# Moving weight and value loads, and splitting the first evacuation and the last accumulation, in a two-layer transformer kernel on one core

## The chip, the core and the metric

The kernel runs on one NeuronCore of a Trainium2 chip. The metric is the device time of one execution in microseconds. Times that are quoted as medians come from several executions; a profile is one execution, and its span (first to last event on the core) was 1.8 us shorter than the time of that same execution (1626.7 and 1628.48). All runs are fast: none was more than 1.5% above the fastest of its kernel.

Engines are named as the profile names them: PE is the tensor engine (matmuls), PEld its weight loads, DVE the vector engine, ACT the scalar engine, SP the engine that issues nearly all DMA transfers here, in program order (in the profile of before, all but two loads of `x`, 384 KB in sum, which ACT issues).

## The reference

Two identical layers run on 2048 tokens of width 1024, in bfloat16 (2 bytes a number). Each layer is attention and then a gated feed-forward block, each with a layernorm ahead and a residual add behind:

```python
def _A_ref(x, wqkv, wo):            # 32 heads of 32, window of 8 keys, 2 apart
    q, k, v = ...                   # (x @ wqkv), split
    kg, vg = k[..., idx, :], v[..., idx, :]        # idx = pos - (0, 2, ..., 14)
    logits = einsum("bhsd,bhswd->bhsw", q, kg) * scale     # masked where idx < 0
    o = einsum("bhsw,bhswd->bhsd", softmax(logits), vg)
    return o @ wo                   # (heads put back side by side)
def _B_ref(x, w1, w3, w2):          # width 3584
    return (silu(x @ w1) * (x @ w3)) @ w2
x = x + _A_ref(layernorm(x), A_wqkv, A_wo); x = x + _B_ref(layernorm(x), B_w1, B_w3, B_w2)
# ... and the same two lines once more
```

## The kernel before

PE does the matmuls. DVE does the whole windowed attention (multiplications and trees of additions), the norms and the residual adds. Tokens go in four chunks of 512; attention works on halves of a chunk (256 tokens). The program first makes q, k and v of chunks 0 to 3 of layer 0 (tile `ps`), with DVE doing attention of chunk 0 beside it; in chunk 3, four output projections (`po`) of chunk 0 are put between the `ps` matmuls; then the first feed-forward stage begins (`pg`, `pu`, then `acc`).

Instruction order on each engine is fixed when the program is built. A small model of time in the builder (`now`, `background`) decides where DVE's attention steps and the output projections go among the matmuls. A change of when a load is expected therefore also moves instructions.

q, k and v go through DRAM (`qkv_d`), since attention needs them in another cut. The value load is tried at the start of a half, when v is often not ready, and again after the softmax:

```python
for g, (l, h) in enumerate(halves):
    load_qk(l, h)
    ...
    load_v(l, h)                       # does nothing if v is not computed yet
    ...
    yield 0.0, ready, lambda: None
    yield from tree(W, mul_qk, lambda w_: psm[:, w_, :])       # scores
    NE = TCH // 32 * 8
    # ... softmax, 20 steps ...
    if g + 1 < len(halves):
        load_qk(*halves[g + 1])        # the next half's q and k
    load_v(l, h)                       # this half's v, behind them in the queue
```

The norm of the first four row blocks of chunk 0 is the program's start. PE transposes each normalized block into a tile that the program places in PSUM (`pT`), and ACT and DVE copy it from there to `xnT`, which the first `ps` matmuls read. These copies are called evacuations. `warm(n)` puts dummy matmuls between, so that PE isn't idle:

```python
kn = KT if j < 2 else KT // 2          # blocks per copy: 8, 8, 4, 4
...
copy = nc.vector.tensor_copy if h else nc.scalar.copy
```

The last accumulation of the program (12 matmuls of 512 columns), its residual add and its store are the program's end.

Of the kernel before, what the change touches and what calls it, by code (L numbers as in the profile page):

```python
# [15 lines left out]
def kernel(  # L16
# [13 lines left out]
    nc = tc.nc  # L30
# [58 lines left out]
    def pe(n, ready=0.0):  # L89
        now["pe"] = max(now["pe"], ready) + n * MM  # L90
        return now["pe"] + 0.1
# [52 lines left out]
    def bank(name):  # L144
        return psum.tile([P, 512], FP32, name=name, tag="mm")
# [24 lines left out]
    def warm(n):  # L170
        for i in range(n):
            pw = bank("pw")
            nc.tensor.matmul(pw[:], lhsT=hT[:, 0, 0:P], rhs=hT[:, 0, :], start=True, stop=True)
# [59 lines left out]
    def ln_first(key):  # L233


        xnT = xnTs[key] = xtp.tile([P, KT, CH], BF16, name="xnT")
        last = TPC - 1
        st = small.tile([P, last, 2, 6], FP32, name="st1", bufs=1)
        mv = small.tile([P, last, 2], FP32, name="mv1", bufs=1)
        sd = small.tile([P, TPC], FP32, name="sd1", bufs=1)  # L240
        rstd = small.tile([P, TPC], FP32, name="rstd1", bufs=1)
        am = small.tile([P, 3], FP32, name="am", bufs=1)
        junk = xnp.tile([P, D], BF16, name="xn")

        def stats(j, hh):
            nc.vector.bn_stats(st[:, j, hh, :], x_sb[:, j, hh * 512:(hh + 1) * 512])

        def deviation(j):
            if j < last:
                nc.vector.bn_aggr(mv[:, j, :], st[:, j, :, :])  # L250
                nc.scalar.activation(sd[:, j:j + 1], mv[:, j, 1:2], ACTF.Sqrt, bias=epst[:])
            else:
                nc.scalar.activation(sd[:, j:j + 1], am[:, 2:3], ACTF.Sqrt, bias=epst[:], scale=1.0 / D)

        def apply(j):
            nc.vector.reciprocal(rstd[:, j:j + 1], sd[:, j:j + 1])
            xn = xnp.tile([P, D], BF16, name="xn")
            if j < last:
                nc.vector.tensor_scalar(xn[:], x_sb[:, j, :], mv[:, j, 0:1], rstd[:, j:j + 1],
                                        op0=ALU.subtract, op1=ALU.mult)  # L260
            else:
                nc.vector.tensor_scalar(xn[:], x_sb[:, j, :], am[:, 1:2], rstd[:, j:j + 1],
                                        op0=ALU.add, op1=ALU.mult)
            kn = KT if j < 2 else KT // 2
            pTs = []
            for k0 in range(0, KT, kn):
                pT = psum.tile([P, kn, P], BF16, name="pT", tag="mm")
                for kk in range(k0, k0 + kn):
                    nc.tensor.transpose(pT[:, kk - k0, :], xn[:, kk * P:(kk + 1) * P], ident[:])
                pTs.append(pT)  # L270
            return pTs

        def evacuate(j, pTs):
            kn = KT // len(pTs)
            for h, pT in enumerate(pTs):
                copy = nc.vector.tensor_copy if h else nc.scalar.copy
                copy(xnT[:, h * kn:(h + 1) * kn, j * P:(j + 1) * P], pT[:])  # L277

        warm(NWARM)
        with hp(), tc.manual_schedule(engines={mybir.EngineType.PE, mybir.EngineType.DVE,  # L280
                                               mybir.EngineType.Activation}):
            stats(0, 0)
            stats(0, 1)
            deviation(0)
            stats(1, 0)
            nc.scalar.activation(junk[:], x_sb[:, last, :], ACTF.Copy, accum_out=am[:, 0:1])
            nc.scalar.mul(am[:, 1:2], am[:, 0:1], -1.0 / D)
            pT0 = apply(0)
            warm(4)
            stats(1, 1)  # L290
            deviation(1)
            nc.scalar.activation(junk[:], x_sb[:, last, :], ACTF.Square, bias=am[:, 1:2], accum_out=am[:, 2:3])
            stats(2, 0)
            pT1 = apply(1)
            warm(4)
            evacuate(0, pT0)
            deviation(last)
            stats(2, 1)
            deviation(2)
            evacuate(1, pT1)  # L300
            pT2 = apply(2)
            warm(2)
            pT3 = apply(3)
            evacuate(2, pT2)
            evacuate(3, pT3)
# [50 lines left out]
    def attention_steps():  # L356
# [3 lines left out]
        for g, (l, h) in enumerate(halves):  # L360
# [13 lines left out]

            yield 0.0, ready, lambda: None
            yield from tree(W, mul_qk, lambda w_: psm[:, w_, :])
            NE = TCH // 32 * 8
            psmT = smp.tile([P, W * NE, 4], BF16, name="psmT", tag="tr")
            L = smp.tile([P, W, NE], FP32, name="L", tag="L")
# [147 lines left out]
    def q_part(l, c, which, ws, then=()):  # L527

        ready = ready_norm(("Q", l, c))
        xnT = xnTs[("Q", l, c)]  # L530
        first = (l, c) == (0, 0) and which < 2
        if first:
            now_T = qkvp.tile([P, KT, TCH + (HALO if which else 0)], BF16, name="kT" if which else "qT")
            firsts.append(now_T)
            if which:
                nc.vector.memset(now_T[:, :, 0:HALO], 0.0)
        for t0 in range(0, KT, SG):
            sgt = stg.tile([P, SG, CH], BF16, name="sgt")
            for t in range(t0, t0 + SG):
                ps = bank("ps")  # L540
                for kk in range(KT):
                    nc.tensor.matmul(ps[:], lhsT=ws[kk // KH][:, kk % KH, t::KT], rhs=xnT[:, kk, :],  # L542
                                     start=(kk == 0), stop=(kk == KT - 1))
                r = pe(KT, ready)
                background(r)
                nc.scalar.copy(sgt[:, t - t0, :], ps[:])  # L546
                done = act(0.6, r)
                if first:
                    nc.scalar.copy(now_T[:, t, HALO if which else 0:], ps[:, 0:TCH])
                    done = act(0.4)  # L550
            nc.sync.dma_start(qkv_d[l][which][:, t0:t0 + SG, c * CH:(c + 1) * CH], sgt[:])
            between(False)
            if then and t0 // SG < len(then):
                then[t0 // SG]()
        qkv_at[l, c, which] = done + DMA / 2
        if len(firsts) == 2:
            qks[0, 0] = firsts[0], firsts[1], done + 0.1
            firsts.append(None)

    def b_stage(u, hold):  # L560
# [5 lines left out]
        for (f0, f1) in fsplits:  # L566
# [32 lines left out]
            for hh in range(2):  # L599
                w2ts = [weight("w2") for g0 in range(f0, f1, 8)]  # L600
                for j in range(TPC):
                    n = c * TPC + j
                    acc = bank("acc")
                    for f in range(f0, f1):
                        nc.tensor.matmul(acc[:], lhsT=hT[:, f - f0, j * P:(j + 1) * P],  # L605
                                         rhs=w2ts[(f - f0) // 8][:, (f - f0) % 8, :],
                                         start=(f == f0), stop=(f == f1 - 1))
                    pe(f1 - f0 - 1)
                    r = pe(1, th)
                    background(r + 1.0)  # L610
                    xs = x_sb[:, n, hh * 512:(hh + 1) * 512]
                    nc.vector.tensor_tensor(xs, xs, acc[:], op=ALU.add)  # L612
                    dve(0.64, r)
                    if last and lastsplit:
                        nc.sync.dma_start(xout[:, n, hh * 512:(hh + 1) * 512], xs)
                    if j == TPC - 1:
                        release(2)
                    between(hold and not lastsplit, lastsplit and hh == 0 and j == 1 and not hold)
# [15 lines left out]
    for c in range(NCH):  # L634
        for which in range(3):
            if c == NCH - 1 and which == 0:
                o_queue += [(0, n) for n in range(TPC)]
            if c == NCH - 1 and which == 2:
                between(False, True)
            then = ()  # L640
            if c == 0 and which == 0:
                then = (lambda: load_x(2), load_weight, load_weight, lambda: load_x(3))
            if c == 1 and which == 0:
                then = (load_weight, load_weight)
            if c == 1 and which == 1:
                then = (lambda: nc.sync.dma_start(wo[:], wo_v),)
            q_part(0, c, which, w_tiles[2 * which:2 * which + 2], then)
            if c == NCH - 1:
                release(2)
            if which == 0 and 1 <= c < NCH - 1:  # L650
                for r in range(R):
                    queue_norm(("Q", 0, c + 1), c + 1, r, (norm_apply,))
# [44 lines left out]
```

## Time and profile before

| reading | value | view |
|---|---|---|
| time, median of 3 | 1627.4 us (1626.39 to 1627.97) | runs |
| span of the profiled run | 1626.7 us | page |
| first projection matmul starts | 13.04 us | timeline of PE |
| one 512-column matmul to the next, streaming | 0.2158 us | timeline of PE |
| matmuls of 512 columns from there on | 7424, worth 1602 us | program |
| end of the last matmul to end of span | 3.5 us | timeline |

So only about 8 us of the stretch between the first and the last of these matmuls is not a stream of matmuls. Busy time doesn't show where it is lost. First, the waits of PE (who waited for whom: total in us, how often, longest).

```profile
PE po L500 <- DVE oT L319: 4.0, 2, 2.0
PE pT L269 <- DVE xn L259: 1.4, 2, 0.8
PE pw L173 <- DVE hT L166: 1.2, 1, 1.2
PE ps L542 <- ACT xnT L277: 0.5, 1, 0.5
```

The last three are in the first 13 us. The first is the third output projection. Its input `oT`, the output of attention, comes in eight slices, one for each matmul of an accumulation. Here it is in the timeline of PE (start, length, engine, line, operation, output and inputs, number; in brackets the idle time just before and what ended it).

```profile
164.98 1.34 PE L500 MATMUL po<-wo,oT 128*128 128x512 bf16 x5
168.33 0.39 PE L500 MATMUL po<-wo,oT 128*128 128x512 bf16 x1 [2.01 <-DVE oT L319]
170.73 4.68 PE L500 MATMUL po<-wo,oT 128*128 128x512 bf16 x10 [2.01 <-DVE oT L319]
...
200.26 1.89 PE L584 MATMUL pg<-xnT,w1t 128*128 128x512 bf16 x8
```

From 164.98 to the first `pg` at 200.26 lie 128 matmuls, which take 27.6 us when they stream. They took 35.3: the stall costs 7.65 us, although the waits name only 4.0. The table by windows shows the rest (window, its length, then busy us and count of PE, PEld, DVE, ACT and POOL, then the granted clock, that is, the clock at which PE was let run, as a share of full speed, DMA share and GB/s).

```profile
150.00:164.98 14.98, 14.87 (x69) 9.68 (x69) 14.80 (x29) 4.28 (x8) 0.00 (x0) 1.00 0.07 24
164.98:170.10 5.12, 1.73 (x7) 0.48 (x5) 5.05 (x10) 1.38 (x3) 0.00 (x0) 1.00 0.87 199
170.20:176.90 6.70, 6.11 (x14) 2.13 (x15) 6.63 (x13) 0.00 (x0) 0.00 (x0) 0.50 1.06 341
177.00:185.00 8.00, 7.95 (x38) 4.57 (x38) 6.80 (x12) 1.21 (x3) 0.00 (x0) 1.00 0.38 112
```

PE counts as 91% busy between 170.2 and 176.9, and yet it does half the work. The busy share doesn't show it; the clock column does, and so do the counts (15 weight loads in 6.7 us, and 38 in the 8.0 us after it). From 171.79 to 176.91 a weight load, and so a matmul, starts every 0.427 us (timeline of PEld), where the stream has one every 0.2158.

Why was `oT` late? DVE, which makes it, had waited for the values 90 us earlier (timeline of DVE, then of the DMA queue on SP).

```profile
80.93 0.11 DVE L335 MEMSET vT<- 128x64 uint32 x1
92.63 1.23 DVE L431 TENSOR_TENSOR tm<-At,vT 128x2048 bf16<-128x2048 bf16 x1 [11.59 <-DMA vT<-qkv_d]
```

```profile
76.44 0.47 SPq L646 DMA_DIRECT2D wo<-in_A_wo_dram  x1
77.00 2.82 SPq L551 DMA_DIRECT2D qkv_d<-sgt  x2
79.87 0.63 SPq L338 DMA_DIRECT2D qT<-qkv_d  x1
80.56 3.87 SPq L338 DMA_DIRECT2D kT<-qkv_d  x1
84.47 2.87 SPq L336 DMA_DIRECT2D vT<-qkv_d  x1
```

The value load is issued at 84.47, behind 2 MB of `wo` and behind q and k of the next half, and lands 8.1 us later. From 92.6 to 171 DVE is busy nearly all the time (76.4 of 78.4 us) and never catches up.

The start of the program, in the timeline of PE, is the third place:

```profile
11.98 0.61 PE L269 MATMUL pT<-ident,xn 128*128 128x128 bf16 x8
13.04 1.24 PE L542 MATMUL ps<-xnT,wqkv 128*128 128x512 bf16 x4 [0.45 <-ACT xnT L277]
```

The last entry of DVE before the end is the last residual add:

```profile
1623.23 0.69 DVE L612 TENSOR_TENSOR x_sb<-x_sb,acc 128x512 bf16<-128x512 bf16 x1 [1.90 <-PE acc L605]
```

### The profile page before, as it was taken

The page shows a single profiled execution, that of the slowest core. Times are in us where ns is not written, and L with a number is a line of the kernel's source. Part 1 is how long each engine was busy: PE and PEld are TensorE (multiplying, and loading weights), DVE is VectorE, ACT ScalarE, POOL GpSimd, SP SyncE. Part 2 cuts the span into 40 slices and gives each one's busy share as a digit, 9 for nine tenths or more (in the row PEclk, how much of TensorE's full clock was granted, in tenths as well). Part 3 has the DMA queues.
Part 4 walks back from the last instruction along what each step waited for, and adds up shares of the span by engine and source line. Part 5 has one row for each costly group of instructions (what it writes and reads, how often), then busy time and mean ns, then how long its engine had stood idle before and what let it go on. Part 6 is the DMA issues. An engine that isn't in the chain of part 4 may idle for free.

```text
span 1626.7 us, 18858 instructions
## 1 busy us (share of the span) xinstructions
PE 1608.2 (99%) x7330; PEld 801.3 (49%) x7479; DVE 1174.2 (72%) x1960; ACT 357.0 (22%) x558; POOL 1.9 (0%) x12
## 2 busy tenths in 40 slices
PE   9999899999999999999999999999999999999999
PEld 5666444444445644455444554445544444444444
DVE  5979998989898989998998439984489943122222
ACT  5432321123012330123312123021230212011110
POOL 0000000000000000000000000000000000000000
PEclk9999999999999999999999999999999999999999
DMA  9644766466547855577563676537775365436540
GB/s 316 185 148 117 209 194 184 139 184 183 169 130 213 254 155 168 168 203 240 157 182 130 207 233 167 178 124 239 227 208 162 99 194 169 142 104 220 156 129 27
DMA packets 335178, 285.28 MB, mean 175 GB/s; under 512 B 69616, under 2 KB 317680, under 8 KB 334960
## 3 DMA queue, kind: packets, MB, share of 16 engines
q1 hardware_dynamic: 334800, 283.67, 57.6%
q8 instruction: 58, 0.95, 0.2%
q10 hardware_dynamic: 288, 0.39, 0.1%
q14 instruction: 32, 0.26, 0.1%
HBM read 238.94 MB, written 29.36 MB: 165 GB/s over the span
## 4 chain that ended last, share of the span: by engine, by line
PE 93%; DVE 5%; DMA 1%; issue 1%; SPq 0%; ACT 0%; DVEq 0%
PE pu L592 24%; PE acc L605 24%; PE pg L584 24%; PE ps L542 15%; PE po L500 6%; DVE tm L431 1%; DVE tm L317 1%; DVE pr L372 1%; DMA vT<-qkv_d 0%; DVE pr L317 0%; SPq L338 0%; DMA x_sb<-in_A_x_dram 0%; DVE oT L319 0%; DVE xn L217 0%; DVE x_sb L505 0%
## 5 line engine op out<-in xcount | busy, mean ns | idle before, releaser
L592 PE MATMUL pu<-xnT,w3t 128*128 128x512 bf16 x1760 | 420.8, 379 | 2.1
L584 PE MATMUL pg<-xnT,w1t 128*128 128x512 bf16 x1751 | 419.2, 379 | 1.8
L605 PE MATMUL acc<-w2t,hT 128*128 128x512 bf16 x1757 | 387.7, 379 | 1.8
L542 PE MATMUL ps<-xnT,wqkv 128*128 128x512 bf16 x1506 | 332.1, 380 | 2.0 <-ACT xnT L277 0.5
L588 ACT ACTIVATE sg<-pg 128x512 bf16<-128x512 f32 x224 | 133.6, 597 | 767.3 <-PE pg L584 708.8
L596 DVE TENSOR_TENSOR hT<-sg,pu 128x512 bf16<-128x512 bf16 x224 | 152.7, 682 | 186.1 <-PE pu L592 174.2
L605 PEld LDWEIGHTS <-hT 128*128 128x128 bf16 x1792 | 175.4, 98 | 211.4
L584 PEld LDWEIGHTS <-w1t 128*128 128x128 bf16 x1792 | 175.4, 98 | 211.4
L592 PEld LDWEIGHTS <-w3t 128*128 128x128 bf16 x1792 | 175.3, 98 | 211.4
L542 PEld LDWEIGHTS <-wqkv 128*128 128x128 bf16 x1536 | 220.5, 144 | 113.0 <-issue 2.1
L372 DVE TENSOR_TENSOR pr<-qT,kT 128x2048 bf16<-128x2048 bf16 x128 | 156.3, 1221 | 88.6 <-DMA kT<-qkv_d 86.6
L431 DVE TENSOR_TENSOR tm<-At,vT 128x2048 bf16<-128x2048 bf16 x128 | 156.3, 1221 | 18.8 <-DMA vT<-qkv_d 16.5
L612 DVE TENSOR_TENSOR x_sb<-x_sb,acc 128x512 bf16<-128x512 bf16 x128 | 87.2, 681 | 103.3 <-PE acc L605 98.4
L546 ACT CAST sgt<-ps 128x512 bf16<-128x512 f32 x192 | 109.8, 587 | 236.5 <-PE ps L542 191.9
L317 DVE TENSOR_TENSOR pr<-pr 128x1024 bf16<-128x1024 bf16 (+1 forms) x256 | 134.5, 552 | 0.5
L317 DVE TENSOR_TENSOR tm<-tm 128x1024 bf16<-128x1024 bf16 (+1 forms) x256 | 134.2, 551 | 0.3
L500 PE MATMUL po<-wo,oT 128*128 128x512 bf16 x501 | 117.7, 384 | 4.7 <-DVE oT L319 4.0
L500 PEld LDWEIGHTS <-oT 128*128 128x128 bf16 x512 | 50.4, 99 | 66.1 <-DVE oT L319 5.6
L192 DVE BATCH_NORM_STATS2 st<-x_sb 128x6 f32<-128x512 bf16 x120 | 76.0, 672 | 6.9 <-DMA x_sb<-in_A_x_dram 6.9
L505 DVE TENSOR_TENSOR x_sb<-x_sb,po 128x512 bf16<-128x512 bf16 x64 | 43.3, 684 | 19.2 <-PE po L500 18.1
L588 ACT ACT_TABLE_LOAD x31 | 39.8, 1283 | 50.8 <-PE pg L584 46.6
L393 DVE STREAM_TRANSPOSE psmT<-psm 128x2048 bf16<-128x2048 bf16 x16 | 36.9, 2307 | 0.2
(88 smaller groups left out, 376.9 us busy)
## 6 DMA issues: line engine op xcount, KB each, us to landing
w1t<-in_B_w_dram SPq DMA_DIRECT2D x56, 1024.0 KB, 5.4
w3t<-in_B_w_dram SPq DMA_DIRECT2D x56, 1024.0 KB, 7.9
w2t<-in_B_w_dram SPq DMA_DIRECT2D x48, 1024.0 KB, 5.3
wqkv<-in_A_wqkv_dram SPq DMA_DIRECT2D x28, 1024.0 KB, 6.6
qkv_d<-sgt SPq DMA_DIRECT2D x96, 256.0 KB, 3.3
w2t<-in_B_w_dram SPq DMA_DIRECT2D x16, 512.0 KB, 5.1
qT<-qkv_d SPq DMA_DIRECT2D x15, 512.0 KB, 9.0
kT<-qkv_d SPq DMA_DIRECT2D x14, 544.0 KB, 9.8
```

The source lines that it names most:

```text
L317: nc.vector.tensor_tensor(b[:, 0:m, :], b[:, 0:m, :], b[:, m:2 * m, :], op=ALU.add)
L372: V.tensor_tensor(pr[:], qT[:], kT[:, :, k0:k0 + TCH], op=ALU.mult)
L431: V.tensor_tensor(tm[:], At[:], win, op=ALU.mult)
L500: nc.tensor.matmul(ps[:], lhsT=oT[:, t, j * P:(j + 1) * P], rhs=wo[:, t, hh * 512:(hh + 1) * 512], start=(t == 0), stop=(t == KT - 1))
L542: nc.tensor.matmul(ps[:], lhsT=ws[kk // KH][:, kk % KH, t::KT], rhs=xnT[:, kk, :], start=(kk == 0), stop=(kk == KT - 1))
L546: nc.scalar.copy(sgt[:, t - t0, :], ps[:])
L584: nc.tensor.matmul(pg[:], lhsT=w1t[:, kk, fi * P:(fi + 1) * P], rhs=xnT[:, kk, :], start=(kk == 0), stop=(kk == KT - 1))
L588: nc.scalar.activation(sg[:], pg[:], ACTF.Silu)
L592: nc.tensor.matmul(pu[:], lhsT=w3t[:, kk, fi * P:(fi + 1) * P], rhs=xnT[:, kk, :], start=(kk == 0), stop=(kk == KT - 1))
L596: nc.vector.tensor_tensor(hT[:, f - f0, :], sg[:], pu[:], op=ALU.mult)
L605: nc.tensor.matmul(acc[:], lhsT=hT[:, f - f0, j * P:(j + 1) * P], rhs=w2ts[(f - f0) // 8][:, (f - f0) % 8, :], start=(f == f0), stop=(f == ...
L612: nc.vector.tensor_tensor(xs, xs, acc[:], op=ALU.add)
```

## The change

Its intent: take weights that aren't needed yet out of the way of the values, ask for the values earlier, start the first projection sooner, and shorten the end. The diff, shortened: re-indented lines and most of its context are left out, and `# ...` marks what else is:

```diff
 # first norm: blocks per copy 8, 8, 8, 2 and another order
-            kn = KT if j < 2 else KT // 2
+            kn = (KT, KT, KT, KT // 4)[j]
-                copy = nc.vector.tensor_copy if h else nc.scalar.copy
+                copy = nc.vector.tensor_copy if j == 2 or h > 1 else nc.scalar.copy
-            evacuate(0, pT0)
             deviation(last)
             stats(2, 1)
             deviation(2)
+            evacuate(0, pT0)
             evacuate(1, pT1)
+            warm(2)
             pT2 = apply(2)
-            warm(2)
             pT3 = apply(3)
 # attention
             yield from tree(W, mul_qk, lambda w_: psm[:, w_, :])
+            load_v(l, h)
 # last accumulation, in two halves of 256 columns (`final` is true once)
+                    step = 256 if final else 512
+                    for q0 in range(0, 512, step):
+                        acc = psum.tile([P, step], FP32, name="acc", tag="mm")
+                        # ... 12 matmuls, add and store of these columns
 # loads beside the projections (one entry after each of the four groups of a part)
-            if then and t0 // SG < len(then):
+            if t0 // SG < len(then) and then[t0 // SG]:
                 then[t0 // SG]()
 # ...
-            if c == 1 and which == 0:
-                then = (load_weight, load_weight)
-            if c == 1 and which == 1:
-                then = (lambda: nc.sync.dma_start(wo[:], wo_v),)
+            if c == 2 and which == 0:
+                then = (None, None, lambda: nc.sync.dma_start(wo[:], wo_v))
+            if c == 2 and which == 1:
+                then = (load_weight, None, load_weight)
```

More of the change, by code (lines that the diff above doesn't have):

```diff
@@ L602, in b_stage @@
                     n = c * TPC + j
-                    acc = bank("acc")
-                    for f in range(f0, f1):
-                        nc.tensor.matmul(acc[:], lhsT=hT[:, f - f0, j * P:(j + 1) * P],
-                                         rhs=w2ts[(f - f0) // 8][:, (f - f0) % 8, :],
-                                         start=(f == f0), stop=(f == f1 - 1))
-                    pe(f1 - f0 - 1)
-                    r = pe(1, th)
-                    background(r + 1.0)
-                    xs = x_sb[:, n, hh * 512:(hh + 1) * 512]
-                    nc.vector.tensor_tensor(xs, xs, acc[:], op=ALU.add)
-                    dve(0.64, r)
-                    if last and lastsplit:
-                        nc.sync.dma_start(xout[:, n, hh * 512:(hh + 1) * 512], xs)
+                    final = u == len(units) - 1 and lastsplit and hh == 1 and j == TPC - 1
+                    step = 256 if final else 512
+                    for q0 in range(0, 512, step):
+                        acc = psum.tile([P, step], FP32, name="acc", tag="mm")
+                        for f in range(f0, f1):
+                            nc.tensor.matmul(acc[:], lhsT=hT[:, f - f0, j * P:(j + 1) * P],
+                                             rhs=w2ts[(f - f0) // 8][:, (f - f0) % 8, q0:q0 + step],
+                                             start=(f == f0), stop=(f == f1 - 1))
+                        if q0 == 0:
+                            pe(f1 - f0 - 1)
+                            r = pe(1, th)
+                            background(r + 1.0)
+                            dve(0.64, r)
+                        o0 = hh * 512 + q0
+                        xs = x_sb[:, n, o0:o0 + step]
+                        nc.vector.tensor_tensor(xs, xs, acc[:], op=ALU.add)
+                        if last and lastsplit:
+                            nc.sync.dma_start(xout[:, n, o0:o0 + step], xs)
                     if j == TPC - 1:
```

## The prediction

> **What bounds it.** TensorE. The page gives PE busy 99%, and the chain of waits that ended last is 93% PE. 7424 512-column matmuls at one per 0.2158 us (the trace's spacing) are 1602 us. The span is 1626.7: 13.04 before the first projection matmul, 1610.4 to the last matmul's end (1623.4), 3.3 of tail. So only 8.2 us inside the matmul stretch are not streaming. Waits of PE show one stall there: "po <- DVE oT", 4.0 us, near 166 to 171 us. The table by windows shows the granted clock at 0.50 from 170.4 to about 177, while po and ps go on at half rate. From the start of that output projection (164.98) to the first gate matmul (200.26) lie 128 matmuls, worth 27.6 us; they took 35.3. The stall therefore costs 7.65 us: 4 idle, 3.6 slow clock. [...]
>
> **Why oT is late.** VectorE is late: it idles 11.6 us (80.9 to 92.6) for vT, whose load stands in the DMA queue behind 2 MB of wo and behind qT and kT; after that VectorE is the chain up to 171.
>
> **What the change does.**
> 1. vT of the first half is now issued after the second chunk-1 query store (about 62.5 us) with w1, w3 and wo out of the way; lands about 70. VectorE reaches it at 81: the 11.6 us wait goes. wo (issued near 105, needed at 140) and w1/w3 (near 112 to 118, needed near 195) come in time.
> 2. The model that orders the program moves too: the third output projection stands one SG group (16 matmuls, 3.45 us) earlier, and one attention tree step (2.4 us) moves ahead of the first residual adds. Replaying trace durations, oT's last slice is ready near 160.5; PE starts that projection near 160.6 and needs the slice at 162. No stall, but only 1 to 2 us to spare. Gain 7.6.
> 3. First norm: sd of rows 2 no longer waits behind the first 0.99 us evacuation, so xn2, xn3 and the transposes come about 0.35 earlier; quarters let the first matmul start after a short copy. First projection matmul near 12.2 instead of 13.04. Gain 0.8 (ScalarE now runs the two big copies back to back, which limits it).
> 4. Tail: 12 extra matmuls, each half the width, about +0.05; last add 256 wide, 0.42 instead of 0.69, and a smaller last store. Gain 0.3 to 0.4.
> 5. Second layer: order shifts on VectorE, values loads earlier; PE had no wait there, so nothing.
>
> All gains lie on the critical path and add: 7.6 + 0.8 + 0.35 = 8.8. 1627.4 - 8.8 = 1618.6 us, range 1617.2 to 1621.3. Faster by over 2% 0.01, within 2% 0.985, slower by over 2% 0.005.
>
> **What would show it.** Right: no "tm <- DMA vT" wait near 81; no (or under 0.5 us) "po <- oT" wait; granted clock 1.00 throughout; first projection matmul at 12.0 to 12.4; first gate matmul near 191.8; last add about 0.4 us. Wrong: a po wait surviving at 160 to 165, PE waiting for wo near 140 or for w1 near 192, first matmul still near 13.
>
> **What would make it wrong.** VectorE's adds wait for po in the new order, so oT comes 2 us later than replayed and a stall of 1 to 3 us stays, perhaps with the half clock again (result 1621 to 1624). Stores held up behind the 2 MB wo load. A new order in the second layer that makes PE wait. The 256-column matmuls not hiding their weight loads (+0.3).

The sum: 7.6 + 0.8 + 0.35 = 8.8, and the 7.6 is read from the trace (35.28 less 27.62 us). The +0.05 for the halved matmuls and the +0.3 for their weight loads are guesses that name no source. Measured after the change, the adds of the two halves start 1.30 us after the add before them and 1.32 us apart (1612.19, 1613.49, 1614.81): 2.62 us for 24 matmuls of 256 columns, where 24 halves of 0.2158 make 2.59.

## The result, and the profile after

| | before | after |
|---|---|---|
| time, median | 1627.68 us (4 runs, 1626.39 to 1628.26) | 1619.63 us (4 runs, 1619.56 to 1619.73) |
| span of the profiled run | 1626.7 us | 1617.9 us |
| first projection matmul | 13.04 us | 12.20 us |
| first `pg` matmul | 200.26 us | 191.80 us |
| end of last matmul to end of span | 3.51 us | 3.13 us |

The ratio of times is 0.9952, with a 95% interval of 0.9934 to 0.9969: about 0.5% less, the class "same" by the 2% rule. A ratio is the mean time of one kernel's fast runs over that of the other's of the same rounds, so it isn't quite the ratio of the medians quoted.

The waits of PE after the change have no `po` line any more (line numbers are one higher from the attention on):

```profile
PE pw L173 <- DVE hT L166: 1.2, 1, 1.2
PE pT L269 <- DVE xn L259: 0.6, 1, 0.6
PE ps L543 <- DVE xnT L277: 0.3, 1, 0.3
```

The same places in the timeline of PE:

```profile
12.20 2.13 PE L543 MATMUL ps<-xnT,wqkv 128*128 128x512 bf16 x8 [0.33 <-DVE xnT L277]
...
160.72 3.62 PE L501 MATMUL po<-wo,oT 128*128 128x512 bf16 x15
164.18 3.62 PE L543 MATMUL ps<-xnT,wqkv 128*128 128x512 bf16 x16
...
191.80 1.89 PE L585 MATMUL pg<-xnT,w1t 128*128 128x512 bf16 x8
```

The third projection streams, and so does what follows; the windows show full clock:

```profile
160.72:164.18 3.46, 3.41 (x17) 1.61 (x17) 2.28 (x3) 0.59 (x1) 0.00 (x0) 1.00 0.85 248
164.18:171.08 6.90, 6.90 (x33) 3.87 (x32) 6.02 (x10) 1.17 (x2) 0.00 (x0) 1.00 1.02 340
```

The cause is gone where it began. The values are issued at 61.94 and land 4.5 us later, and DVE has no wait in front of its first multiplication with them (queue of SP, then DVE):

```profile
61.94 0.62 SPq L336 DMA_DIRECT2D vT<-qkv_d  x1
```

```profile
80.19 1.23 DVE L432 TENSOR_TENSOR tm<-At,vT 128x2048 bf16<-128x2048 bf16 x1
...
160.19 0.29 DVE L319 TENSOR_TENSOR oT<-tm 128x256 bf16<-128x256 bf16 x1
...
1613.49 0.42 DVE L619 TENSOR_TENSOR x_sb<-x_sb,acc 128x256 bf16<-128x256 bf16 x1 [0.62 <-PE acc L609]
1614.81 0.42 DVE L619 TENSOR_TENSOR x_sb<-x_sb,acc 128x256 bf16<-128x256 bf16 x1 [0.89 <-PE acc L609]
```

The last slice of `oT` is done at 160.48, 0.2 us before the projection that reads it starts and 1.7 us before its own matmul, the eighth (160.72 and seven times 0.2158). The last add takes 0.42 instead of 0.69 us.

### The profile page after: what moved, and what is told of

The parts are those of the page before. It is cut to its first block, busy times and chain, and to the rows that moved or that the text cites. A ratio compares the mean times of both kernels' runs of the same rounds, so it can differ in the third digit from the quotient of the medians.

```text
span 1617.9 us, 18887 instructions
## 1 busy us (share of the span) xinstructions
PE 1604.7 (99%) x7342; PEld 802.1 (50%) x7491; DVE 1176.1 (73%) x1962; ACT 358.8 (22%) x558; POOL 1.9 (0%) x12
## 4 chain that ended last, share of the span: by engine, by line
PE 98%; DVE 1%; issue 1%; DMA 0%; ACT 0%; SPq 0%; DVEq 0%
PE acc L609 24%; PE pu L593 23%; PE pg L585 23%; PE ps L543 20%; PE po L501 7%; DVE tm L432 0%; DMA x_sb<-in_A_x_dram 0%; DVE tm L317 0%; DVE hT L597 0%; DVE st L246 0%; DVE At L416 0%; DVE xn L259 0%; ACT xnT L277 0%; DVE xnT L277 0%; PE pT L269 0%
## 5 line engine op out<-in xcount | busy, mean ns | idle before, releaser
L609 PE MATMUL acc<-w2t,hT 128*128 128x512 bf16 (+1 forms) x1769 | 387.7, 378 | 1.8
L319 DVE TENSOR_TENSOR psm<-pr 128x256 bf16<-128x256 bf16 x128 | 36.7, 287 | 0.5
```

The costliest lines, as they stand in the source:

```text
L609: nc.tensor.matmul(acc[:], lhsT=hT[:, f - f0, j * P:(j + 1) * P], rhs=w2ts[(f - f0) // 8][:, (f - f0) % 8, q0:q0 + step], start=(f == f0), ...
```

## The experiments

Theory: nearly all of the gain is one stall, caused by the wait of DVE for the values, and it costs its idle time plus a period at half clock; head and tail add about 1.1 us on top. Rivals: the traffic of the weights and not the place of the value load is the cause; or the clock drop has another origin and only the waiting counts; or head and tail gains are eaten by later waits.

Since the first matmul's start moves by a few tenths from run to run with the landing of the first input (in the seven profiles with the head of the change it lies between 11.78 and 12.46, and always 6.19 to 6.25 after the first `xn`, which came at 5.58 to 6.21; DVE's waits ahead of that name the load of `x`), spans are compared below from the first projection matmul on, where that matters. The profile gives spans to 0.1 us, so such a difference is good to about 0.1 us.

| run | time, median us (lowest to highest) | span | first `ps` | span from first `ps` | `po` wait of PE | half clock |
|---|---|---|---|---|---|---|
| before | 1627.40 (1626.39 to 1627.97) | 1626.7 | 13.04 | 1613.66 | 4.0 | 170.2 to 177.0 |
| e1 values early | 1620.55 (1620.36 to 1620.55) | 1618.8 | 12.76 | 1606.04 | none | none |
| e2 weights later | 1622.02 (1621.60 to 1623.10) | 1619.8 | 12.52 | 1607.28 | 0.3 | none |
| e3 filled stall | 1625.79 (1625.14 to 1626.37) | 1623.8 | 12.95 | 1610.85 | 1.0 | none |
| e11 head and tail | 1626.57 (1626.14 to 1627.12) | 1625.1 | 12.33 | 1612.77 | 4.0 | 168.1 to 174.9 |
| e4 after again | 1619.48 (1619.47 to 1619.59) | 1617.7 | 11.97 | 1605.73 | none | none |
| e5 old head | 1620.22 (1620.18 to 1620.28) | 1618.5 | 12.84 | 1605.66 | none | none |
| e6 old tail | 1619.85 (1619.67 to 1620.12) | 1617.8 | 11.80 | 1606.00 | none | none |
| e7 finer both | 1619.77 (1619.27 to 1620.47) | 1617.9 | 11.56 | 1606.34 | none | none |
| e8 one more | 1619.49 (1619.46 to 1619.51) | 1617.7 | 11.98 | 1605.72 | none | none |
| e9 three more | 1621.60 (1621.59 to 1622.05) | 1620.3 | 12.46 | 1607.84 | 1.8 | none |
| e10 six more | 1628.02 (1627.19 to 1628.51) | 1625.4 | 11.78 | 1613.62 | 5.3 | 165.1 to 171.9 |
| e12 finer head | 1619.40 (1619.16 to 1619.43) | 1617.6 | 11.96 | 1605.64 | none | none |

e1, e2, e3 and e11 ran on one chip, where before had 1627.70; e4 to e7 together, with before at 1627.79; e8 to e10 together, with before at 1627.48; e12 alone, with before at 1627.13. All results were correct.

### e1: only the values earlier

```diff
 # the kernel before, with
             yield from tree(W, mul_qk, lambda w_: psm[:, w_, :])
+            load_v(l, h)
```

> The kernel before with only the new place of the values load (after the scores); wo, w1, w3 still load in chunk 1. Theory (the 11.6 us wait of VectorE for vT is the whole cause of the stall, and the place of the load in the queue is enough): the vT wait near 81 us is gone or under 1 us, no po <- oT wait, granted clock 1.00, span 7.6 us under that of before (1626.7), so about 1619. Rival (traffic of w1, w3 and wo is what delays vT): the wait for vT stays above 5 us, the stall stays, gain under 4 us.

The stall and the wait are gone although `w1`, `w3` and `wo` still load in chunk 1: from the first `ps` on the span is 1606.04, which is 7.6 us less than before (1613.66 less 1606.04). The value load is issued at 62.96, right behind 2 MB of `w1` and `w3`, and lands only after 8.2 us, as slowly as before (8.1). That doesn't matter, because DVE wants it at 80.7. The rival that traffic alone is the cause falls: being asked for 18 us early is enough. The edit also lets the builder's model put the third projection 16 matmuls earlier (161.25), as in the changed kernel, so e1 doesn't change the load alone; e2, which leaves the order as it was, shows that the new order isn't needed to lose the stall.

### e2: only the weights later

```diff
 # the kernel before, with the guard of `then` as in the change, and
-            if c == 1 and which == 0:
-                then = (load_weight, load_weight)
-            if c == 1 and which == 1:
-                then = (lambda: nc.sync.dma_start(wo[:], wo_v),)
+            if c == 2 and which == 0:
+                then = (None, None, lambda: nc.sync.dma_start(wo[:], wo_v))
+            if c == 2 and which == 1:
+                then = (load_weight, None, load_weight)
```

> The kernel before with only wo, w1, w3 moved into chunk 2; order of PE, VectorE, ScalarE unchanged, vT still issued after qT and kT. Theory (queue place and traffic each are enough): vT issued near 81, lands near 87, VectorE's wait 6 to 7 instead of 11.6 us, so oT about 5 us earlier, the stall at the third output projection 0 to 1 us and no half clock: gain 6.5 to 7.6 us. Rival (the queue place alone matters): wait for vT above 10 us, stall and half clock stay, gain under 1 us.

The order on PE, DVE and ACT is that of before. The values were issued at 80.77 and DVE's wait fell from 11.6 to 7.3 us, where 6 to 7 had been worked out; the `po` wait fell to 0.3 and the clock stayed at full speed. So traffic alone was also enough to lose the stall; the rival of the queue place alone falls too. But the gain in the median was 5.7 us (1627.70 less 1622.02), and 6.4 in the profiles from the first `ps` on, less than the 6.5 to 7.6 expected. A new wait shows, which the expectation hadn't seen:

```profile
193.38 1.89 PE L584 MATMUL pg<-xnT,w1t 128*128 128x512 bf16 x8 [0.56 <-issue]
```

The first feed-forward matmul reads `xnT` and `w1t`. `w1t` of this stage was issued at 121.8, long before. The last two transposes of `xnT` were issued only at this point in the DMA queue, behind 2 MB of weights issued from 181.79 on:

```profile
181.79 0.42 SPq L471 DMA_DIRECT2D w1t<-in_B_w_dram  x1
182.31 1.67 SPq L471 DMA_DIRECT2D w3t<-in_B_w_dram  x1
184.06 7.05 SPq L220 DMA_TRANSPOSE xnT<-xn  x2
```

The two transposes took the queue 7.05 us to issue, until 191.1. In the changed kernel the builder's model, which expects the values earlier, also puts the third and fourth output projections 16 matmuls earlier, and with them the adds and the norm; the same two transposes were issued from 176.09 on, in 2.69 us, 13 us before they were wanted. The second of the two was issued at 188.6 and took 4.5 us to land, until 193.1, 0.3 us before `pg` started. That the transposes are what `pg` waited for is read from their place and these times; the profile names no releaser, and no run took this wait away by itself. From the start of the third projection (164.47) to `pg`, e2 takes 1.3 us more than its 128 matmuls need: 0.55 for the last slice of `oT` (its matmul starts at 166.53) and the rest at `pg`. That is what e2 falls short of e1 from the first `ps` on (1607.28 less 1606.04).

### e3: the stall filled with dummy matmuls

```diff
 # the kernel before, in the output projection
         oT = oTs[l, h]
+        if (l, n) == (0, 2):
+            warm(16)
         for hh in range(2):
```

> The kernel before with 16 dummy matmuls (3.45 us) put just ahead of the third output projection, where PE would idle. Theory (the stall costs 4.0 us of idling and 3.6 us of half clock): granted clock stays 1.00, idle left under 1 us, the first gate matmul about 3.6 us earlier than before's 200.26, span near 1623.1. Rival (the cost is only the waiting, or the slow clock comes from something else such as power or DMA load): the first gate matmul stays at 200 or moves later by up to 3.4 us, and the clock drops in the same place.

Sixteen useless matmuls made the kernel faster: 1625.79 against 1627.70. The clock stayed at 1.00:

```profile
164.89 3.62 PE L173 MATMUL pw<-hT 128*128 128x512 bf16 x16
168.34 1.46 PE L502 MATMUL po<-wo,oT 128*128 128x512 bf16 x6
170.54 0.39 PE L502 MATMUL po<-wo,oT 128*128 128x512 bf16 x1 [0.73 <-DVE oT L319]
```

So the clock drop goes with PE being idle, and not with the DMA load of that time, which this run has too (DMA share 0.84 from 165.0 to 168.4 and 0.91 to 1.06 from there to 172.0, in windows of e3). The first `pg` was at 197.33, 2.93 us earlier than before, not 3.6, and from the first `ps` on the run was 2.8 us shorter. The expectation had taken the waiting from the list of waits, which ends with the next-to-last slice of `oT`. In the kernel before the last slice's matmul starts at 171.39 (its weight load is at that time in the timeline of PEld) and would have started at 166.49 if the projection had streamed from 164.98. So waiting costs 4.9 us. The half clock then lasts to 177.0 and costs half of the 5.6 us from there, 2.8. Together that is, within 0.1 us, the 7.65 that was read, and 2.8 is what e3 saved. The split of the prediction, 4 and 3.6, was wrong and its sum was right.

### e11: only head and tail

```diff
 # the kernel before, with
-            kn = KT if j < 2 else KT // 2
+            kn = (KT, KT, KT, KT // 4)[j]
 # ... and the other lines of the first norm in the change
+                    step = 256 if final else 512
 # ... and the loop over q0 of the change
```

> The kernel before with only the new first norm and the halved last accumulation. Theory (the parts add up): first projection matmul near 12.20 instead of 13.04, tail 0.3 us shorter, stall as in before; if VectorE in chunk 0 moves with PE, the stall stays near 4 us: gain 1.1 us in the span, and times vary between runs as those of before do. Rival: the earlier start makes PE reach the stall 0.84 us earlier while oT comes no earlier (VectorE's wait is set by the DMA queue), so the head's gain is eaten by a stall 0.84 us longer: gain only 0.3 us.

The gain in the median is 1.13 us (1627.70 less 1626.57), with the `po` wait unchanged at 4.0. The rival of a longer stall falls, but for a little: DVE's work moved with PE's, and the last slice's matmul (170.87) came 5.05 us late, where it was 4.9 before. The half clock fell differently (windows of this run):

```profile
165.80:168.00 2.20, 0.19 (x1) 0.10 (x1) 2.17 (x5) 0.37 (x1) 0.00 (x0) 1.00 1.06 199
168.10:174.90 6.80, 4.74 (x12) 1.64 (x12) 6.73 (x12) 0.00 (x0) 0.00 (x0) 0.50 1.04 327
```

The same stall now meets the drop 2.3 us after its beginning, not 3.8 as before, so the slow period covers 4.0 us of streaming work after the last slice (170.87 to 174.9) and not 5.6. Its cost is 2.0 and not 2.8 us. The cost of nearly the same stall thus varies with the moment at which the clock drops, 170.2 in before and 168.1 here.

### e4, e5, e6: the changed kernel again, with the old head, with the old tail

```diff
 # e5: the changed kernel with
-            kn = (KT, KT, KT, KT // 4)[j]
+            kn = KT if j < 2 else KT // 2
 # ... and the other lines of the first norm as before
 # e6: the changed kernel with
-                    step = 256 if final else 512
+                    step = 512
```

> The changed kernel again, as the base of the next three runs. Expected 1619.6 us with a spread under 0.4 us between runs, while the kernel before spreads over 1.5 to 2 us [...].

> The changed kernel with the old first norm. Theory: first projection matmul at 13.0 instead of 12.2, span 0.8 us longer (1618.7), time 1620.4. Rival (the head's gain is hidden by later waits): within 0.2 us of the changed kernel.

> The changed kernel with the old, unhalved last accumulation. Theory: last add 0.69 instead of 0.42 us and a larger last store: 0.2 to 0.4 us longer (span 1618.1 to 1618.3). Rival (extra matmuls and an extra store eat it): within 0.1 us or shorter.

The old head costs 0.74 us (1620.22 less 1619.48), all of it ahead of the first matmul: from there on the spans are 1605.66 and 1605.73. The old tail costs 0.37 in the medians, and 0.27 in the span from the first `ps` (1606.00 less 1605.73); the time from the last matmul's end is 3.46 and 3.15. Both rivals fall. The repeat of the changed kernel gave the same time within 0.15 us, with a spread of 0.12.

### e7 and e12: finer pieces

```diff
 # e7 and e12: the changed kernel with
-            kn = (KT, KT, KT, KT // 4)[j]
+            kn = (KT, KT, KT // 2, KT // 4)[j]
 # e7 only
-                    step = 256 if final else 512
+                    step = 128 if final else 512
```

> The changed kernel with the second-last evacuation of the first norm in halves (one on ScalarE, no: both by VectorE) and the last accumulation in quarters. Theory: the first projection matmul now waits for VectorE's 0.69 us copy; its half lets it start about 0.25 us earlier (near 11.95), and quarters save another 0.1 us of add and store: 0.2 to 0.4 us faster. Rival: ScalarE's two big copies set the start, so nothing at the head, and 128-wide matmuls are bound by their weight loads, so the tail loses 0.1 us or more.

> The changed kernel with the third row block of the first norm evacuated by VectorE in two halves, the last accumulation in halves as in the changed kernel. Theory (the first projection matmul waits for VectorE's 0.69 us copy of eight blocks, of which it needs one; the earlier run with quarters started earlier and lost that at the tail): first projection matmul 0.2 to 0.3 us earlier, no wait for a VectorE copy before it, tail as in the changed kernel, median 1619.2 to 1619.3 against 1619.5. Rival (that earlier start was only jitter of when the first input lands): 1619.5, same as the changed kernel.

e7 missed its expectation: the median is 0.3 us above the changed kernel's (1619.77 against 1619.48), not 0.2 to 0.4 below. Its head did gain (2.00 us from `xn` of the third block to the first `ps`, as in e12 below). The last add became shorter and the end longer: 3.74 us from the last matmul's end against 3.15. Matmuls weren't the cause; the DVE timeline shows three adds 0.67 us apart, so the 12 matmuls of 128 columns of each took 56 ns apiece. By the column that is within 4% of the 215.8 ns for 512 columns, so weight loads held them up by little at most.

```profile
1612.86 0.29 DVE L619 TENSOR_TENSOR x_sb<-x_sb,acc 128x128 bf16<-128x128 bf16 x1 [0.38 <-PE acc L609]
1613.53 0.29 DVE L619 TENSOR_TENSOR x_sb<-x_sb,acc 128x128 bf16<-128x128 bf16 x1 [0.38 <-PE acc L609]
1614.20 0.29 DVE L619 TENSOR_TENSOR x_sb<-x_sb,acc 128x128 bf16<-128x128 bf16 x1 [0.38 <-PE acc L609]
```

The stores were: the four of 32 KB took 3.7, 3.4, 2.9 and 2.4 us from issue to landing, where the two of 64 KB in the changed kernel took 1.5 and 1.6. The rows of the four are 256 bytes. What made the stores slow isn't shown: the 128 KB store just ahead of them, whose rows have 1024 bytes, also took 3.9 us where the others of its size took 1.7 (the eleven stores from 1596.7 on: 1.7 at least, 1.8 in the median, 3.9 at most). No run separates the row size from there being five stores close together.

e12 keeps the halves. Measured from DVE's `xn` of the third block (10.00 in the changed kernel, 9.96 here) to the first `ps`, the head takes 2.00 instead of 2.20 us, and the wait of `ps` for a DVE copy is gone:

```profile
11.96 1.24 PE L543 MATMUL ps<-xnT,wqkv 128*128 128x512 bf16 x5
```

The median is 1619.40 against 1619.48 and 1619.63 for the changed kernel, in other rounds. That is 0.1 to 0.2 us, in the direction of the theory and of a size that the landing of the first input can also make. So the shorter head is seen in the profile, but it isn't settled that the time is shorter by more than jitter.

### e8, e9, e10: delaying DVE on purpose

```diff
 # the changed kernel; N = 1, 3 or 6 repeats ahead of the last slices of oT
-                V.tensor_tensor(tm[:], At[:], win, op=ALU.mult)
+                for _ in range(N + 1 if (l, h, t) == (0, 1, 7) else 1):
+                    V.tensor_tensor(tm[:], At[:], win, op=ALU.mult)
```

> The changed kernel with one repeated 128x2048 multiply (1.2 us) in VectorE's work just ahead of oT's last slices of the first chunk's second half. Theory (1.7 us of slack: last slice ready near 160.5, wanted near 162.2): no po wait over 0.1 us, span unchanged within 0.2 us. Rival (no slack left, PE just did not show the wait): 1 us longer.

> The same with three repeated multiplies (about 3.5 us). Theory: a po wait of about 1.8 us; [...] granted clock 1.00 and the span 1.8 us longer, near 1619.7. Rival: clock drops too and the span is 4 to 5 us longer.

> The same with six repeated multiplies (about 7 us). Theory: about 5.2 us of po waiting, [...] the clock falls to half for 5 to 7 us and costs another 2.5 to 3.6 us: span 8 to 9 us longer, near 1626. Rival (only waiting counts): 5.2 us longer, clock 1.00.

One repeat cost nothing (1605.72 against 1605.73 from the first `ps`): the slack that the prediction worked out is there. Three cost 2.1 us with a `po` wait of 1.8 and full clock. Six brought back the loss of the kernel before, 7.9 us from the first `ps` (1613.62 less 1605.73), just under the 8 to 9 expected. The list of waits has 5.3 of it:

```profile
PE po L502 <- DVE oT L319: 5.3, 1, 5.3
```

```profile
165.10:166.90 1.80, 0.00 (x0) 0.00 (x0) 1.80 (x5) 0.00 (x0) 0.00 (x0) 0.50 0.00 0
167.02:171.70 4.68, 4.62 (x11) 1.63 (x12) 3.00 (x5) 0.00 (x0) 0.00 (x0) 0.50 0.75 240
```

The clock fell while PE waited, with the DMA engines at rest (share 0.00), and stayed at 0.50 until 171.9. Counted as in e3, the last slice's matmul came 5.9 us late (167.68 by its weight load; 161.82 when streaming from 160.31), and the half clock cost half of the 4.2 us from there, 2.1. Waiting alone accounts for 5.9 of 7.9, so the rival falls here too. In all three profiles with a drop the half clock lasted 6.8 us: 170.2 to 177.0, 168.1 to 174.9 and 165.1 to 171.9. It began 3.8 (before), 2.3 (e11) and 3.3 us (e10) after the stream of matmuls broke off, in before and e11 with one matmul inside that time. With 1.0 (e3) and 1.8 us (e9) of waiting the clock stayed at 1.00. What sets the moment of the drop, and what ends the half clock, isn't shown.

## Why the prediction was right

1. **The stall and its cost (7.6 us): right in sum, mis-sized in its parts.** e1 alone gives 7.6. The step "4 idle, 3.6 slow clock" should have been 4.9 of waiting and 2.8 of slow clock (e3). The list of waits shows 4.0 because the 0.44 us that the last slice's matmul lost stood between half-rate matmuls, and because the list counts idle time from the modelled end of a matmul, 0.39 us after its start, where the next one would stream after 0.2158: that hides 0.17 us in each of the two waits. The prediction's 6.5 us of half clock was 6.8 in windows of 0.1 us.
2. **The cause (values behind `wo`, q and k): right, with an addition.** Either cure alone removes the stall (e1, e2). Asking for the values early brings 7.1 us in the medians (1627.70 less 1620.55) and moving the weights 5.7. What they bring together isn't their sum: once e1 is in, moving the weights had little left to give (1606.04 less 1605.73, and most of that 0.31 is the tail).
3. **The slack ("1 to 2 us to spare"): right.** e8 spent 1.25 us of it for nothing. In e9 the four multiplications took 5.00 us instead of 1.23; this delay of 3.8 us cost 2.1, so 1.7 of it was slack.
4. **Head (0.8): right.** e5 gives 0.74. The 0.84 in the two profiles holds about 0.1 of jitter: the first `xn` came at 6.12 before and 6.00 after, and 6.92 against 6.20 us lie between it and the first `ps`. The remark that ACT's two big copies limit the start was wrong: the first `ps` waited for DVE's copies (0.33), and halving DVE's copy of the third block took that wait away and 0.2 us off the head (e12).
5. **Tail (0.3 to 0.4): right.** 3.51 to 3.13 in the profiles, 0.27 to 0.37 by e6. (The prediction read 3.3 before; the timeline has the last matmul's end at 1623.2, not 1623.4.)
6. **Second layer (nothing): right.** From 300 to 1500 us, PE is as busy in both tables by windows as it was (1194.10 us before, 1194.16 after).
7. **The time, 1618.6 against 1619.63 measured: in the range, 1.0 us low.** The gain in spans, 8.8 us, is the number predicted. The step that failed is subtracting it from the median of 1627.4: it was read from a profiled execution that itself took 1628.48, 1.1 us more than that median. The gain between medians was 8.05.

Why before varies by over 2 us (1626.26 to 1628.70 in all its runs) and the changed kernel by less than 0.3 is partly seen: the half clock of nearly the same stall cost 2.8 us in the profile of before and 2.0 in that of e11. The mean granted clock that is recorded for each run agrees. Of the 32 runs of before beside the experiments, the 19 with 0.998 took 1627.28 to 1628.70, 1628.0 in the mean, and the 13 with 0.999 took 1626.26 to 1627.39, 1626.7 in the mean: runs that lost less clock were 1.2 us shorter in the mean. But e2, e3 and e7, with a clock of 1.0 in every run, also spread by 1.2 to 1.5 us, so the clock isn't all of it, and what else there is stays open.

## What to carry to other kernels

When an engine in front of the bottleneck is late, look far upstream: the loss at 165 us came from a load that stood in the wrong place in a queue at 80 us, and asking for it as soon as its buffer and data allowed cured it even behind 2 MB of weights (e1). Price a stall of PE from the distance between two fixed matmuls, less the streaming time of the matmuls between, and not from the list of waits; here that was 7.65 against 4.0. Read a gain against the time of the execution that was profiled, not against the median of others.
